# Six slices of w_in shared by three groups, and PSUM as two rings of two, in a retention and SiLU kernel

## The chip, the cores and the metric

The kernel runs on one core of one Trainium2 chip. The time is the device time of the core in microseconds, and lower is better. Three runs of the kernel before gave 663.20, 664.37 and 661.12 us, so its median is 663.2 us.

## The reference

The first part is a recurrent retention over 4 batches, 8 heads, 768 positions and a head dimension of 64. The second part is a dense block with a SiLU between two products, over 3072 tokens of width 512, with an inner width of 2048.

```python
gamma = 1.0 - 2.0 ** (-5.0 - np.arange(H))
for t in range(S):
    state = gamma * state + einsum('bhd,bhe->bhde', k[:, :, t], v[:, :, t])
    y[:, :, t] = scale * einsum('bhd,bhde->bhe', q[:, :, t], state)
x = y.transpose(0, 2, 1, 3).reshape(B * S, H * D)
h = x @ w_in
g = h * (1.0 / (1.0 + np.exp(-h)))
out = g @ w_out
```

## The kernel before

**Retention in chunks.** The 768 positions are cut into 6 chunks of 128. One chunk of one batch is a unit, so there are 24 units, taken in the order of chunks. A unit passes through three steps on TensorE, at three successive visits. `stage_t` transposes k and q into PSUM, and ACT copies them out as `kt` and `qt`. `stage_a` forms the scores `sc` from them, and VectorE multiplies these by the decay into `am`. `stage_y` forms the unit's output y from v and `am` and from q and the running state, and adds k times v to the state. So visit m does the transpositions of unit m, y of unit m - 2 and the scores of unit m - 1, in that order. `finish_y` and `split_x` then turn y into x of the dense block. All the x of one chunk, for its four batches, is a group of 512 tokens.

**Three-term products.** The dense products run in the fp32r format. Each operand is held as three parts: a high part, a low part, and a mix of both. In the code these are indices 0, 1 and 2. A product of x and a slice of w_in is 12 matmuls: for each of the four parts of the inner dimension, high by high and low by low go to the accumulator `ha`, and mix by mix goes to `hb`. At the end ACT takes `ha` into a tile of the pool `hpool`, VectorE subtracts `hb`, ACT applies the SiLU, and the tile g is stored to DRAM.

**The slices of w_in.** There are 16 slices of 128 columns (index f). The weights come as 64-bit words. `take_w` takes the next slice: it asks for a load two slices ahead, converts the words to 32 bits on VectorE and ACT (`convert_w`), and splits the result in three (`split_w`). After the 16 slices of w_in it goes on with the 16 slices of w_out, which are only converted and stored to DRAM. The output stage needs them later.

**The order of the work.** Six visits come first, with four slices. Then a list of phases says which groups use which slices. Groups 0 and 1 use slices 0 to 7 in turn, then group 0 and group 1 use slices 8 to 15. Between the products the list places the takes of slices and the visits. Groups 2 to 5 then go over all 16 slices each, with visits and w_out conversions in between. The output stage reads g back from DRAM, splits it in three (`split`), and multiplies it by w_out with eight accumulators, two for each batch.

**Group 2's x.** The pool `xpool` has two places. Group 2's x (`LATE`) is made while groups 0 and 1 hold both. So `finish_y` copies y of this chunk to an SBUF tile `ys` and stores it to DRAM, and `late_x` loads it back (`yr`) and splits it. The four calls of `late_x` stand after products (1, 9), (1, 10), (1, 11) and (1, 12). The tiles `ys`, `yr` and g share the three buffers of `hpool`, tag `hs`.

**PSUM.** The eight banks are cut up by name. The pool `ps_u` has one buffer each for `s` (two banks, for the transposed k and for the scores), `q` (one bank, for the transposed q) and `y` (two banks). The pool `ps_h` has three banks that `ha` and `hb` take in turn.

**What sets the order.** TensorE does its instructions in the order in which the program is written. For the other engines a scheduler places the instructions, and each engine then does its own in that order, one after another. Loads and stores are issued by SyncE, also in order. Each waits at the head of its queue until its buffer is free and its data is ready. The helper `issue_after` keeps a slice's first ACT step behind a named earlier ACT instruction.

The code around the change follows, with the line numbers that the profile uses.

Of the kernel before, what the change touches and what calls it, by code (L numbers as in the profile page):

```python
# [31 lines left out]
def kernel(  # L32
# [53 lines left out]
    hpool = pool("hpool", 3)  # L86
    stage = pool("stage", 2)
    conv = pool("conv", 1)
    ps_u = pool("ps_u", 1, space=PS)
    ps_h = pool("ps_h", 3, space=PS)  # L90

    g_dram = {(c, f): dram.tile([128, NT], FP32, tag=f"g{c}_{f}", name=f"gd_{c}_{f}")
              for c in range(NC) for f in range(NF)}
# [3 lines left out]
    def bits(x):  # L97
        return float(np.array(x, np.uint32).view(np.float32))

    def split_w(f, w32, name, factor):  # L100

        w = wpool.tile([128, 3, 512], FP32R, tag=f"w{f}", name=f"{name}{f}")
        lo = conv.tile([128, 512], FP32, tag="wl", name=f"{name}l_{f}")
        with tc.issue_after(evac[0]):
            nc.scalar.activation(out=w[:, 0, :], in_=w32, func=AF.Copy, scale=HALF * factor)
        high = w[:, 0, :].bitcast(FP32)
        nc.vector.scalar_tensor_tensor(out=lo, in0=w32, scalar=factor, in1=high,
                                       op0=ALU.mult, op1=ALU.subtract)
        nc.scalar.activation(out=w[:, 1, :], in_=lo, func=AF.Copy, scale=1.0 / EPS)
        nc.vector.scalar_tensor_tensor(out=w[:, 2, :], in0=high, scalar=EPS, in1=lo,  # L110
                                       op0=ALU.mult, op1=ALU.subtract)
        return w
# [73 lines left out]
        nc.vector.tensor_tensor(out=w, in0=s.bitcast(FP32), in1=p.bitcast(FP32), op=ALU.add)  # L186
        return w

    evac, w_sb = [], {}
    taken = [0]  # L190

    def take_w(between=lambda: None):
# [69 lines left out]

    xt, kt, qt, am, live = {}, {}, {}, {}, {}

    def banks(tag, name, n=2):
        return ps_u.tile([128, n, 512], FP32, tag=tag, name=name)

    def turn(name):  # L270
        return ps_h.tile([128, 512], FP32, tag="h", name=name)

    def scale_k(n):
        if 0 <= n < len(units) and units[n][0] < NC - 1:
# [9 lines left out]

    def stage_t(n):

        kp = turn(f"kp_{n}") if n < B + 2 else banks("s", f"kp_{n}")[:, 0]
        qp = banks("q", f"qp_{n}", 1)[:, 0]
        for (name, to, bufs), src, tp in ((("kt", kt, 2), kqv["k"][n], kp),
                                          (("qt", qt, 3), kqv["q"].pop(n), qp)):  # L290
            tp = tp.rearrange("p (a t) -> p a t", a=HP)
            for a in range(HP):
                nc.tensor.transpose(tp[:, a, :], src[:, 2 * a : 2 * a + 2, :], ident)  # L293
            to[n] = one.tile([128, HP, C], FP32, tag=name, name=f"{name}_{n}", bufs=bufs)
            evac[:] = [nc.scalar.copy(out=to[n], in_=tp).ins]

    def stage_y(n):

        c, b = units[n]
        kf, vs = kqv["k"].pop(n), kqv["v"].pop(n)  # L300
        qtn, amn = qt[n], am.pop(n)
        u = banks("y", f"y_{n}")

        yp = u[:, :, : 2 * C].rearrange("p o (i t) -> p i o t", i=2)
        sp = u[:, 1, 2 * C :].rearrange("p (a e) -> p a e", a=HP)

        started = set()

        def product(j, bank, **kw):
            nc.tensor.matmul(start=(j, bank) not in started, skip_group_check=True, **kw)  # L310
# [13 lines left out]
        if c > 0:  # L324
            for i in range(0, HP, 2):
                for a in (i, i + 1):
                    for j in range(2):
                        o = j ^ (a % 2)
                        product(o, a % 2, out=yp[ts(o, D), a // 2, a % 2, :],
                                lhsT=state[b][ts(j, D), a, :], rhs=qtn[ts(j, D), a, :],  # L330
                                stop=True)
        live[n] = sp, yp

    def stage_a(n):

        u = banks("s", f"sc_{n}").rearrange("p j (a t) -> p j a t", a=HP)
        ktn = kt.pop(n)
        for a in range(HP):
            for j in range(2):
                for half in range(2):  # L340
                    nc.tensor.matmul(u[ts(half, D), j, a, :], lhsT=ktn[ts(j, D), a, ts(half, D)],  # L341
                                     rhs=qt[n][ts(j, D), a, :], start=True, stop=True,
                                     skip_group_check=True)
        am[n] = one.tile([128, 2, HP, C], FP32, tag="am", name=f"am_{n}")
        nc.vector.tensor_tensor(out=am[n], in0=u, in1=decay, op=ALU.mult)

    def finish_y(n):
        c, b = units[n]
        sp, yp = live.pop(n)
        qt.pop(n)  # L350
        if b == 0 and c != LATE:
            xt[c] = xpool.tile([128, 3, KIN, NT], FP32R, tag="xt", name=f"xt_{c}")
        if c == LATE:
            y = hpool.tile([128, KIN, C], FP32, tag="hs", name=f"ys_{b}")
            nc.scalar.copy(out=y.rearrange("p (i o) t -> p i o t", o=2), in_=yp)
            nc.sync.dma_start(out=y_dram[b], in_=y)
            rest = None
        else:
            rest = split_x(c, b, yp)
        if c == 0:  # L360
            nc.scalar.copy(out=state[b], in_=sp)
        elif c < NC - 1:
            nc.vector.tensor_tensor(out=state[b], in0=state[b], in1=sp, op=ALU.add)
        return rest

    def split_x(c, b, y):
        xh, xl, xm = (xt[c][:, i, :, ts(b, C)].rearrange("p (i o) t -> p i o t", o=2)
                      for i in range(3))
        nc.scalar.activation(out=xh, in_=y, func=AF.Copy, scale=HALF)
        nc.vector.tensor_tensor(out=xl, in0=y, in1=xh.bitcast(FP32), op=ALU.subtract)  # L370
        return lambda: nc.vector.scalar_tensor_tensor(
            out=xm, in0=xl.bitcast(FP32), scalar=-1.0 / EPS, in1=xh.bitcast(FP32),
            op0=ALU.mult, op1=ALU.add)


    LATE = 2
# [32 lines left out]
    pending = []  # L409

    def product_in(c, f):
        ha, hb = turn(f"ha_{c}_{f}"), turn(f"hb_{c}_{f}")
        for i in range(3):
            for kk in range(KIN):
                nc.tensor.matmul(hb if i == 2 else ha, lhsT=w_sb[f][:, i, ts(kk, 128)],  # L415
                                 rhs=xt[c][:, i, kk, :], start=kk == 0 and i != 1,
                                 stop=kk == KIN - 1 and i != 0)
        hs = hpool.tile([128, NT], FP32, tag="hs", name=f"g_{c}_{f}")
        nc.scalar.activation(out=hs, in_=ha, func=AF.Copy, scale=ONE_E)  # L419
        nc.vector.tensor_tensor(out=hs, in0=hs, in1=hb, op=ALU.subtract)  # L420
# [54 lines left out]
    for m in range(1, B + 2):  # L475
# [2 lines left out]
            take_w()  # L478
        if m == 2:
            first_chunk()  # L480
    half = NF // 2
    phases = ((0, 0, (0, 1, 2, 3, 5), (0, 1, 2, 3, 4, 5, 6)),
              (1, 0, (1, 3, 5), (0, 1, 2, 3, 5)),
              (0, half, (), (2, 6)),
              (1, half, (), (7,)))
    for c, f0, at, takes in phases:
        for i in range(half):
            product_in(c, f0 + i)
            if i in takes:
                take_w()  # L490
            put_g(1)
            if i in at:
                visit()
            if (c, f0) == (1, half) and 1 <= i <= B:
                late_x(i - 1)
    for c in range(2, NC):
        for f in range(NF):
            product_in(c, f)
            if c < NC - 1 and f % 3 == 0:
                take_w()  # L500
            put_g(1)
            if f % 4 == 1:
                visit()
            if c == NC - 1:
                if f == 0:
                    get_w(0)
                    get_w(1)
                wo[f] = split_w(f, w_got.pop(f), "wo", 1.0)
                get_w(f + 2)
                if f >= NF - 6:  # L510
                    if f == NF - 6:
                        for n in range(G_AHEAD):
                            get(n)
                    if f >= NF - S_AHEAD:
                        split(f - NF + S_AHEAD)
    put_g(0)

    for c in range(NC):
        acc = []
        for b in range(B):  # L520
            if b < 2:
                u = banks("sy"[b], f"o{b}_{c}")
                acc.append([u[:, i] for i in range(2)])
            else:
                acc.append([turn(f"oa{b}_{c}"), turn(f"ob{b}_{c}") if b == 2 else
                            banks("q", f"ob{b}_{c}", 1)[:, 0]])
        for f in range(NF):
            n = c * NF + f
            split(n + S_AHEAD)
# [45 lines left out]
```

## Time and profile before

| what | value |
|---|---|
| median of three runs | 663.2 us |
| the profiled execution, its time | 663.2 us |
| the profiled execution, its span | 661.1 us |
| TensorE matmul (PE) busy | 630.0 us, 95% |
| TensorE weight load (PEld) busy | 517.8 us, 78% |
| VectorE (DVE) busy | 422.4 us, 64% |
| ScalarE (ACT) busy | 283.1 us, 43% |
| granted TensorE clock, mean | 0.99 |
| DMA, mean | 157 GB/s |

The span is the stretch from the first to the last instruction of the profiled execution. Busy times of engines overlap, so they do not add up. In the lists of waits a line names the waiting instruction, the instruction or transfer that released it, the total in microseconds, how often it was seen, and the longest. In a timeline a line has the start, the time taken, the engine, the line of the code and the operation, and in square brackets the idle time before it and what ended it. Matmuls are pipelined, so that the time from the start of one to the start of the next is shorter than what is given as the duration of one.

### The profile page before, as it was taken

What the parts mean: (1) busy time and instruction counts of PE and PEld (TensorE: products, weight loads), DVE (VectorE), ACT (ScalarE), POOL (GpSimd) and SP (SyncE); (2) the same over time, 40 slices, a digit from 0 to 9 for tenths busy, and PEclk for the clock granted to TensorE, in tenths of its full rate; (3) what the DMA queues carried; (4) which work ended last, traced back from release to release, by engine and by line L of the source; (5) the groups of instructions that cost most, each with busy time, mean ns of one, the idle gap of its engine ahead of it and who ended that gap; (6) DMA issues with size and microseconds to landing.
All of it is one profiled execution on the core that took longest, in us unless ns stands there. A gap on an engine that the chain in (4) does not pass through costs nothing.

```text
span 661.1 us, 11067 instructions
## 1 busy us (share of the span) xinstructions
PE 630.0 (95%) x4288; PEld 517.8 (78%) x4288; DVE 422.4 (64%) x696; ACT 283.1 (43%) x510; POOL 12.6 (2%) x44
## 2 busy tenths in 40 slices
PE   3878979899999999999999999999999999999996
PEld 2667758688888888888888888888888888888885
DVE  4999998995568787864348775454464545554631
ACT  5465546564554444444438881222131412222311
POOL 3000100100000000000000000000000000000000
PEclk9989989999999999999999999999999999999999
DMA  8957866867457775864326654252343443423401
GB/s 192 226 129 200 205 199 194 222 223 223 144 168 218 197 216 160 243 205 160 128 81 191 195 181 134 77 179 81 110 146 110 130 126 95 160 95 96 153 7 63
DMA packets 123060, 103.48 MB, mean 157 GB/s; under 512 B 80000, under 2 KB 88192, under 8 KB 123008
## 3 DMA queue, kind: packets, MB, share of 16 engines
q1 hardware_dynamic: 119552, 96.49, 49.9%
q10 hardware_dynamic: 3456, 6.29, 2.6%
q8 instruction: 33, 0.54, 0.3%
q14 instruction: 19, 0.16, 0.1%
HBM read 66.06 MB, written 36.70 MB: 155 GB/s over the span
## 4 chain that ended last, share of the span: by engine, by line
PE 73%; DVE 0%; ACT 0%; issue 0%; ACTq 0%
PE ha L415 18%; PE hb L415 9%; PE ob L537 7%; PE o L536 7%; PE o L537 7%; PE o L535 7%; PE oa L536 7%; PE oa L535 7%; PE y L310 4%; PE sc L341 1%; PE kp L293 1%; PE qp L293 1%; DVE o L543 0%; ACT o L542 0%; ACT g L419 0%
## 5 line engine op out<-in xcount | busy, mean ns | idle before, releaser
L415 PE MATMUL ha<-xt,wi 128*128 128x512 f32 x768 | 192.9, 393 | 2.9 <-DVE g L420 2.9
L415 PEld LDWEIGHTS ha<-xt,wi 128*128 128x128 f32 x768 | 142.4, 188 | 36.3 <-DVE g L420 3.7
L462 DVE TENSOR_TENSOR gs<-gr,gs 128x512 fp32r<-128x512 f32 x96 | 62.1, 686 | 93.8 <-ACT gs L460 93.8
L460 ACT ACTIVATE gs<-gr 128x512 fp32r<-128x512 f32 x96 | 53.5, 620 | 139.7 <-issue 131.8
L415 PE MATMUL hb<-xt,wi 128*128 128x512 f32 x384 | 104.0, 393 | 3.1 <-ACT g L419 3.0
L420 DVE TENSOR_TENSOR g<-g,hb 128x512 f32<-128x512 f32 x96 | 65.7, 684 | 60.8 <-PE hb L415 43.5
L421 ACT ACTIVATE g<-g 128x512 f32<-128x512 f32 x96 | 60.5, 632 | 70.9 <-DVE g L420 69.2
L415 PEld LDWEIGHTS hb<-xt,wi 128*128 128x128 f32 x384 | 72.3, 189 | 19.3 <-ACT g L419 4.4
L537 PE MATMUL ob<-wo,gs 128*128 128x512 f32 x192 | 75.2, 392 | 0.0
L536 PE MATMUL o<-wo,gs 128*128 128x512 f32 x192 | 74.7, 389 | 0.0
L537 PE MATMUL o<-wo,gs 128*128 128x512 f32 x192 | 74.7, 389 | 0.0
L535 PE MATMUL o<-wo,gs 128*128 128x512 f32 x192 | 74.7, 389 | 0.0
L535 PE MATMUL oa<-wo,gs 128*128 128x512 f32 x192 | 74.7, 389 | 0.0
L536 PE MATMUL oa<-wo,gs 128*128 128x512 f32 x192 | 74.7, 389 | 0.0
L419 ACT ACTIVATE g<-ha 128x512 f32<-128x512 f32 x96 | 56.6, 589 | 40.1 <-PE ha L415 33.3
L463 DVE SCALAR_TENSOR_TENSOR gs<-gs 128x512 fp32r<-128x512 f32 x96 | 61.9, 684 | 0.0
L537 PEld LDWEIGHTS ob<-wo,gs 128*128 128x128 f32 x192 | 36.0, 188 | 9.0 <-DVE o L543 1.7
L535 PEld LDWEIGHTS oa<-wo,gs 128*128 128x128 f32 x192 | 36.0, 188 | 7.7 <-ACT o L542 0.2
L537 PEld LDWEIGHTS o<-wo,gs 128*128 128x128 f32 x192 | 36.0, 188 | 7.5
L536 PEld LDWEIGHTS o<-wo,gs 128*128 128x128 f32 x192 | 36.0, 188 | 7.5
L536 PEld LDWEIGHTS oa<-wo,gs 128*128 128x128 f32 x192 | 36.0, 188 | 7.4
L535 PEld LDWEIGHTS o<-wo,gs 128*128 128x128 f32 x192 | 36.0, 188 | 7.3
(65 smaller groups left out, 612.8 us busy)
## 6 DMA issues: line engine op xcount, KB each, us to landing
gd<-g SPq DMA_DIRECT2D x96, 256.0 KB, 3.1
gr<-gd SPq DMA_DIRECT2D x96, 256.0 KB, 2.7
wf<-in_moe_w_out_dram SPq DMA_DIRECT2D x16, 512.0 KB, 3.9
kf<-in_k_dram SPq DMA_DIRECT2D x24, 256.0 KB, 4.5
qf<-in_q_dram SPq DMA_DIRECT2D x24, 256.0 KB, 4.5
vf<-in_v_dram SPq DMA_DIRECT2D x24, 256.0 KB, 4.5
out_dram<-o ACTq DMA_DIRECT2D x24, 256.0 KB, 2.1
wf<-in_moe_w_in_dram SPq DMA_DIRECT2D x16, 256.0 KB, 3.2
```

The costliest lines, as they stand in the source:

```text
L293: nc.tensor.transpose(tp[:, a, :], src[:, 2 * a : 2 * a + 2, :], ident)
L310: nc.tensor.matmul(start=(j, bank) not in started, skip_group_check=True, **kw)
L415: nc.tensor.matmul(hb if i == 2 else ha, lhsT=w_sb[f][:, i, ts(kk, 128)], rhs=xt[c][:, i, kk, :], start=kk == 0 and i != 1, stop=kk == KIN ...
L419: nc.scalar.activation(out=hs, in_=ha, func=AF.Copy, scale=ONE_E)
L420: nc.vector.tensor_tensor(out=hs, in0=hs, in1=hb, op=ALU.subtract)
L421: nc.scalar.activation(out=hs, in_=hs, func=AF.Silu)
L460: nc.scalar.activation(out=t[:, 0, :], in_=g, func=AF.Copy, scale=HALF)
L462: nc.vector.tensor_tensor(out=t[:, 1, :], in0=g, in1=high, op=ALU.subtract)
L463: nc.vector.scalar_tensor_tensor(out=t[:, 2, :], in0=t[:, 1, :].bitcast(FP32), scalar=-1.0 / EPS, in1=high, op0=ALU.mult, op1=ALU.add)
L535: nc.tensor.matmul(oa, lhsT=gh, rhs=wo[f][:, 0, :], start=first_, stop=False)
L536: nc.tensor.matmul(oa, lhsT=glo, rhs=wo[f][:, 1, :], start=False, stop=last)
L537: nc.tensor.matmul(ob, lhsT=gm, rhs=wo[f][:, 2, :], start=first_, stop=last)
```

## The change

**PSUM.** `ps_u` becomes one tag `u` of two banks with two buffers, which the transpositions of k and q together, the scores and y take in turn. `ps_h` gets the tags `ha` and `hb`, with two buffers each. The output stage takes its accumulators from these.

**Products.** The 12 matmuls are issued with the part of the inner dimension outermost: two on `ha`, one on `hb`, and so on.

**Slices.** The last four slices share one tile, `wq`, of four places. Group 2's x stands in this tile first: `finish_y` still copies y to `ys` and stores it to DRAM, and it now also splits it into the tile. The slices that come into the tile follow the products that read x from it.

**Order.** A dictionary `steps` gives for each product whether a slice is taken and whether a visit follows. Groups 0, 1 and 2 use slices 0 to 5, groups 0 and 1 slices 6 to 10, groups 0 and 1 slices 11 to 15, and group 2 slices 6 to 15. The four calls of `late_x` stand after products (1, 12) to (1, 15).

```diff
-    ps_u = pool("ps_u", 1, space=PS)
-    ps_h = pool("ps_h", 3, space=PS)
+    ps_u = pool("ps_u", 2, space=PS)
+    ps_h = pool("ps_h", 2, space=PS)
...
+    def w_slot(f, name):
+        if f < NF - 4:
+            return wpool.tile([128, 3, 512], FP32R, tag=f"w{f}", name=f"{name}{f}")
+        if f == NF - 4:
+            quads[name] = wpool.tile([128, 4, 3, 512], FP32R, tag="wq", name=f"{name}4")
+        return quads[name][:, f - NF + 4]
...
-        w = wpool.tile([128, 3, 512], FP32R, tag=f"w{f}", name=f"{name}{f}")
+        w = w_slot(f, name)
...
-        with tc.issue_after(evac[0]):
+        with tc.issue_after(held[0] if f >= NF - 4 else evac[0]):
...
-    def banks(tag, name, n=2):
-        return ps_u.tile([128, n, 512], FP32, tag=tag, name=name)
-
-    def turn(name):
-        return ps_h.tile([128, 512], FP32, tag="h", name=name)
+    def banks(name):
+        return ps_u.tile([128, 2, 512], FP32, tag="u", name=name)
...
-        kp = turn(f"kp_{n}") if n < B + 2 else banks("s", f"kp_{n}")[:, 0]
-        qp = banks("q", f"qp_{n}", 1)[:, 0]
-        for (name, to, bufs), src, tp in ((("kt", kt, 2), kqv["k"][n], kp),
-                                          (("qt", qt, 3), kqv["q"].pop(n), qp)):
-            tp = tp.rearrange("p (a t) -> p a t", a=HP)
+        tp = banks(f"tp_{n}").rearrange("p o (a t) -> p o a t", a=HP)
+        for i, src in enumerate((kqv["k"][n], kqv["q"].pop(n))):
             for a in range(HP):
-                nc.tensor.transpose(tp[:, a, :], src[:, 2 * a : 2 * a + 2, :], ident)
+                nc.tensor.transpose(tp[:, i, a, :], src[:, 2 * a : 2 * a + 2, :], ident)
+        for i, (name, to, bufs) in enumerate((("kt", kt, 2), ("qt", qt, 3))):
             to[n] = one.tile([128, HP, C], FP32, tag=name, name=f"{name}_{n}", bufs=bufs)
-            evac[:] = [nc.scalar.copy(out=to[n], in_=tp).ins]
+            evac[:] = [nc.scalar.copy(out=to[n], in_=tp[:, i]).ins]
...
-        if b == 0 and c != LATE:
-            xt[c] = xpool.tile([128, 3, KIN, NT], FP32R, tag="xt", name=f"xt_{c}")
+        if b == 0:
+            p, tag = (wpool, "wq") if c == LATE else (xpool, "xt")
+            xt[c] = p.tile([128, 3, KIN, NT], FP32R, tag=tag, name=f"xt_{c}")
         if c == LATE:
             y = hpool.tile([128, KIN, C], FP32, tag="hs", name=f"ys_{b}")
-            nc.scalar.copy(out=y.rearrange("p (i o) t -> p i o t", o=2), in_=yp)
+            y4 = y.rearrange("p (i o) t -> p i o t", o=2)
+            nc.scalar.copy(out=y4, in_=yp)
             nc.sync.dma_start(out=y_dram[b], in_=y)
-            rest = None
-        else:
-            rest = split_x(c, b, yp)
+            yp = y4
+        rest = split_x(c, b, yp)
...
-        ha, hb = turn(f"ha_{c}_{f}"), turn(f"hb_{c}_{f}")
-        for i in range(3):
-            for kk in range(KIN):
-                nc.tensor.matmul(hb if i == 2 else ha, lhsT=w_sb[f][:, i, ts(kk, 128)],
-                                 rhs=xt[c][:, i, kk, :], start=kk == 0 and i != 1,
-                                 stop=kk == KIN - 1 and i != 0)
+        ha = ps_h.tile([128, 512], FP32, tag="ha", name=f"ha_{c}_{f}")
+        hb = ps_h.tile([128, 512], FP32, tag="hb", name=f"hb_{c}_{f}")
+        for kk in range(KIN):
+            w = [w_sb[f][:, i, ts(kk, 128)] for i in range(3)]
+            x = [xt[c][:, i, kk, :] for i in range(3)]
+            first_, last = kk == 0, kk == KIN - 1
+            nc.tensor.matmul(ha, lhsT=w[0], rhs=x[0], start=first_, stop=False)
+            nc.tensor.matmul(ha, lhsT=w[1], rhs=x[1], start=False, stop=last)
+            nc.tensor.matmul(hb, lhsT=w[2], rhs=x[2], start=first_, stop=last)
...
-    phases = ((0, 0, (0, 1, 2, 3, 5), (0, 1, 2, 3, 4, 5, 6)),
-              (1, 0, (1, 3, 5), (0, 1, 2, 3, 5)),
-              (0, half, (), (2, 6)),
-              (1, half, (), (7,)))
...
-            if (c, f0) == (1, half) and 1 <= i <= B:
-                late_x(i - 1)
...
+    for c, f, takes, at in ((0, range(6), (0, 2, 5), (0, 1, 3, 4)),
+                            (1, range(6), (2, 5), (0, 1, 3, 4)),
+                            (2, range(6), (1, 4), ()),
+                            (0, range(6, 11), (7, 9), ()),
+                            (1, range(6, 11), (7, 9), ()),
+                            (0, range(11, NF), (11, 13), ()),
+                            (1, range(11, NF), (), ()),
+                            (2, range(6, NF), (6, 9, 12, 15), (6, 8, 11, 13))):
+        for i in f:
+            steps[c, i] = i in takes, i in at
+    for c in range(3, NC):
+        for f in range(NF):
+            steps[c, f] = c < NC - 1 and f % 3 == 0, f % 4 == 1
+    for (c, f), (takes, at) in steps.items():
+        product_in(c, f)
+        if takes:
+            take_w()
+        put_g(1)
+        if at:
+            visit()
+        if c == 1 and NF - B <= f:
+            late_x(f - NF + B)
...
-                u = banks("sy"[b], f"o{b}_{c}")
+                u = banks(f"o{b}_{c}")
                 acc.append([u[:, i] for i in range(2)])
             else:
-                acc.append([turn(f"oa{b}_{c}"), turn(f"ob{b}_{c}") if b == 2 else
-                            banks("q", f"ob{b}_{c}", 1)[:, 0]])
+                acc.append([ps_h.tile([128, DM], FP32, tag=f"h{i}", name=f"o{i}{b}_{c}")
+                            for i in "ab"])
```

More of the change, by code (lines that the diff above doesn't have):

```diff
@@ L98, in bits @@
         return float(np.array(x, np.uint32).view(np.float32))
+    quads = {}
+    def w_slot(f, name):
[4 more added lines that the diff above has]
+        return quads[name][:, f - NF + 4]
     def split_w(f, w32, name, factor):
-        w = wpool.tile([128, 3, 512], FP32R, tag=f"w{f}", name=f"{name}{f}")
+        w = w_slot(f, name)
         lo = conv.tile([128, 512], FP32, tag="wl", name=f"{name}l_{f}")
-        with tc.issue_after(evac[0]):
+        with tc.issue_after(held[0] if f >= NF - 4 else evac[0]):
             nc.scalar.activation(out=w[:, 0, :], in_=w32, func=AF.Copy, scale=HALF * factor)
@@ L187, in convert_w @@
         return w
-    evac, w_sb = [], {}
+    evac, held, w_sb = [], [], {}
     taken = [0]
@@ L301, in stage_y @@
         qtn, amn = qt[n], am.pop(n)
-        u = banks("y", f"y_{n}")
+        u = banks(f"y_{n}")
         yp = u[:, :, : 2 * C].rearrange("p o (i t) -> p i o t", i=2)
@@ L334, in stage_a @@
     def stage_a(n):
-        u = banks("s", f"sc_{n}").rearrange("p j (a t) -> p j a t", a=HP)
+        u = banks(f"sc_{n}").rearrange("p j (a t) -> p j a t", a=HP)
         ktn = kt.pop(n)
@@ L368, in split_x @@
                       for i in range(3))
-        nc.scalar.activation(out=xh, in_=y, func=AF.Copy, scale=HALF)
+        held[:] = [nc.scalar.activation(out=xh, in_=y, func=AF.Copy, scale=HALF).ins]
         nc.vector.tensor_tensor(out=xl, in0=y, in1=xh.bitcast(FP32), op=ALU.subtract)
@@ L480 @@
             first_chunk()
-    half = NF // 2
-    phases = ((0, 0, (0, 1, 2, 3, 5), (0, 1, 2, 3, 4, 5, 6)),
-              (1, 0, (1, 3, 5), (0, 1, 2, 3, 5)),
-              (0, half, (), (2, 6)),
-              (1, half, (), (7,)))
[L486 to L493, printed above, removed]
-            if (c, f0) == (1, half) and 1 <= i <= B:
-                late_x(i - 1)
@@ L496 @@
-    for c in range(2, NC):
-        for f in range(NF):
[L498 to L515, printed above, removed]
+    steps = {}
@@ new lines @@
+    for c in range(3, NC):
+        for f in range(NF):
+            steps[c, f] = c < NC - 1 and f % 3 == 0, f % 4 == 1
[8 more added lines that the diff above has]
+            late_x(f - NF + B)
+        if c == NC - 1:
+            if f == 0:
+                get_w(0)
+                get_w(1)
+            wo[f] = split_w(f, w_got.pop(f), "wo", 1.0)
+            get_w(f + 2)
+            if f >= NF - 6:
+                if f == NF - 6:
+                    for n in range(G_AHEAD):
+                        get(n)
+                if f >= NF - S_AHEAD:
+                    split(f - NF + S_AHEAD)
```

## The prediction

> **What bounds the kernel now.** I read the page's slices first, then TensorE's waits by stretch, then the timelines where they fall.
>
> ```profile
> PE   3878979899999999999999999999999999999996
> DVE  4999998995568787864348775454464545554631
> PEclk9989989999999999999999999999999999999999
> ```
>
> Each digit is 16.5 us. TensorE is full from about 130 us on; its holes lie in the first eight slices, where VectorE stands at 9. From 175 us to the end no matmul is listed as waiting. So only what happens before about 130 us can be gained, and whatever stalls TensorE later is lost whole. The waits of TensorE between 33 and 131 us:
>
> ```profile
> PE ha L415 <- DVE g L420: 2.9, 2, 1.5
> PE hb L415 <- ACT g L419: 2.9, 1, 2.9
> PE kp L293 <- DVE am L345: 2.7, 3, 1.1
> PE y L310 <- ACT state L361: 2.6, 1, 2.6
> PE y L310 <- DVE am L345: 1.0, 1, 1.0
> PE sc L341 <- ACT kt L295: 0.3, 2, 0.2
> ```
>
> They all end on ACT or VectorE emptying a bank. What one wait costs shows in TensorE's timeline:
>
> ```profile
> 91.28 1.97 PE L415 MATMUL ha<-xt,wi 128*128 128x512 f32 x8
> 96.13 2.08 PE L415 MATMUL hb<-xt,wi 128*128 128x512 f32 x4 [2.88 <-ACT g L419]
> 98.00 1.06 PE L293 MATMUL kp<-ident,kf 128*128 128x128 f32 x4
> ...
> 113.33 2.11 PE L415 MATMUL ha<-xt,wi 128*128 128x512 f32 x8
> 115.28 1.07 PE L415 MATMUL hb<-xt,wi 128*128 128x512 f32 x4
> ```
>
> After the 2.88 us hole four matmuls take 2.08 us in place of 1.07, and the small ones are slow until about 102.3: some 6.2 us at half rate, about 3.1 us lost on top of the hole. After the hole at 33 to 37 us it is 3.5 us at half rate.
>
> Units of account. In the full stretch a product (12 matmuls) starts every 2.72 us (147.32, 150.04, 152.76). An attention visit adds 4.10 us: hb ends at 180.43 and the product after next starts at 187.25, 6.82 less 2.72. Before, products run from 40.94, and at 130.86 there are 16 products and 8 visits done: 16 x 2.72 + 8 x 4.10 = 76.3 us of work in 89.9. **13.6 us is lost there, and that is all that the front can give.** VectorE explains it: 8 slices of w_in are made ready for the first 8 products. By the pitch of the timeline (0.60 us for a 128x512 of two operands, 0.34 for one, 1.13 for am, 0.33 for state) a slice costs it 4.0 us, a visit 3.9, a product 0.6: 8.5 us for one of each, against 6.8 on TensorE.
>
> Last, the reload of group 2's x, which now has cover:
>
> ```profile
> 163.04 0.69 DVE L370 TENSOR_TENSOR xt<-yr,xt 128x512 fp32r<-128x512 f32 x1 [0.73 <-ACT xt L369]
> ...
> 172.53 0.69 DVE L371 SCALAR_TENSOR_TENSOR xt<-xt 128x512 fp32r<-128x512 f32 x1
> ```
>
> Its fourth part is asked for after product (1,12), which ends at 166.4, and is ready at 173.2: 6.8 us later. Group 2 starts at 174.99, because three products stand in between.
>
> **What the Trainium skill says.** "TensorE: Matmul & The Clock Gate", Part 1, gives half rate after an idle window of about 3.4 us and full rate after a busy one, with a free-running window; the 3.5 and 6.2 us above agree, and say that the cost can be one or two windows. "ScalarE: Activation LUTs", What ACT_TABLE_LOAD costs, gives 1283 ns and a drain of 1380; the trace shows 1.28 us at 45.10 and the next activation at 46.39, so no drain is counted. "DMA: Bandwidth & Descriptors", Anatomy of one DMA, gives about 2 us fixed, so a store followed by a load cannot be short; the trace has 2.7 us median for yr and 3.1 for gd.
>
> **The change, part by part.**
>
> *Order of products: six slices shared by groups 0, 1, 2.* Slices needed early fall from 8 in 16 products to 6 in 18; takes are spread at about one per 2 to 3 products. VectorE per visit and product without a slice is 4.5 us against 6.8. So the standing shortage goes. The same 18 products and 8 visits ended before at 130.86 + 2 x 2.72 = 136.3; without stalls they need 81.8 from 40.94, which is 122.7. New stalls in this stretch:
>
> S1. In the changed program VectorE does am of unit 4 (1.13), a step of slice 3 (0.6) and scale_q (0.6) ahead of the last xm of group 0; before, xm was done at 41.94, ahead of am at 42.46. And the product now takes kk outermost, so its third matmul wants xm, not its ninth. Tp, sc and y share two buffers, so a transposition waits for the state copy of the y two visits back, with no product between in the prologue. Walking the prologue with the durations above: state copies let the transposition of visit 5 go at about 35.7 (before 32.1), y of unit 3 ends at 39.7, am at 42.9, xm at 45.0. The third matmul wanted 41.4: **3.6 us**.
>
> S2. sc of the first visit in group 0 needs qt's copy too (same buffer), which ACT does behind the table load (1.28) and the silu (0.63), and this waits for the subtraction, queued on VectorE behind all of slice 4 (5.1 us chained). sc then starts at about 53.4 where 50.2 is wanted: **3.2 us**, with the half rate after S1 inside it. Later visits: product end E, ha copy to E+0.5, subtraction to E+1.3, silu to E+1.95, qt to E+2.5, sc wanted at E+2.94: covered by y's own 2.1 us, by 0.4. Where a slice step stands in front (visits 8 and 10) I count 0.7 + 1.0 = **1.7 us**.
>
> S3. x of group 2 is now also split at once, from ys; xm stands behind am and scale_q, with one product of cover (2.72): ready about 5.1 after y, wanted at 4.2: **1.0 us**.
>
> Sum 9.5: the 18 products end at 132.2, a **gain of 4.1 us** (13.6 at most).
>
> *Double ha, hb in place of three in turn; banks alternating.* This removes the four waits of hb/ha on g (5.8 us, part of the 13.6). The output stage already alternates banks and runs 12 matmuls per 2.72 us: nothing for the alternation.
>
> *x of group 2 in place of the last four slices.* The spill to DRAM and the reload stay: 4 stores, 4 loads, none saved. ACT and VectorE gain 4 splits (0.63 + 0.69 + 0.69 each, 8.0 us in all), in the stretch just counted. The four slices wait for (2,5); they are wanted from (0,12), over seven products later: covered. The four last wo slices wait likewise for (5,15), and are wanted 12 output steps later, 32 us: covered.
>
> *Reload at f = 12 to 15.* The SyncE order is the same as before, shifted by three products: gd 11, yr, gd 12, yr, gd 13, gd 14, yr, yr. But product (2,6) follows (1,15) at once, where three products (8.2 us) stood. The last yr needs the slot of g(1,14), hence its store landed. Taking the measured chain over: xm ready 6.8 us after (1,15), wanted 0.45 after: **6.4 us**. Bounds: 5.5 if stores land in 2.0; 9 if each takes 3.1, since ACT now places the second yr's xh ahead of silu 14. A hole of 6 us puts the clock at half: 3.5 to 6.2 us of it, 1.7 to 3.1 lost, I take **2.4**. Together **8.8 us**; TensorE has nothing else to do there, its order is written by hand. Behind it q, k, v of later visits wait too, but they have three visits of lead.
>
> *The 12 later visits* with sc behind qt: cover 0.4 us each; bounds 0 and 8, I take **0.5**.
>
> Net: -4.1 + 8.8 + 0.5 = **+5.2 us**: span 666.3. The profiled execution took 663.2 with a span of 661.1, and the median is 663.2 too, so the time is 668.4, in round numbers 668; a slowdown of 0.8%. 0.5%, 3.3 us, is about what can be told from no change.
>
> **Rivals.** *Faster:* the front loses only S1 (3.6): it gains 13.6 - 3.6 = 10.0; the reload costs its lower bound of 5.5 and 0.5 of clock, 6.0: 663.2 - 10.0 + 6.0 = 659.2. For it: all prices of S2 hang on queue order, and half rate may fall inside work that waits anyway. Against: the reload chain is measured. It decides once the front's gain exceeds the reload by 3.3. *A wash:* front gain 7, reload 8: 664. *The ring becomes the bound:* sc waits for qt in most visits, 0.6 us in 16 more of the 24: 668.4 + 9.6 = 678. For it: the cover is 0.4 us and ACT is in order. Against: in the full stretch before, qt's copy ends at 182.66 and sc starts at 183.37.
> *No effect of the sharing:* if the k, q, v transfers set the pace (196 GB/s in 41 to 131 us, 226 at most), the front gains nothing and the time is 672; no such wait is listed after 20 us.
>
> **How the numbers follow.** Forecast case (664.5 to 672.5) 0.54; wash 0.18; faster 0.15; ring or transfers 0.13. The range takes in half of the fast case and of the slow one: 660 to 675. Faster by over 0.5%: 0.14; within: 0.25; slower: 0.61, from forecast and ring, less the forecast's edge below 666.5.
>
> **What would show it.** Product (2,6) starts, and its third matmul waits 5 to 9 us for xm of the last yr, with a slow clock after; the first product waits some 3 us for xm; waits of kp on am vanish; sc on ACT's qt appears. (2,5) ends at about 132. Wrong if (2,6) waits under 3 us, or if (2,5) ends before 127 or after 137.

## The result and the profile after

The changed kernel takes **671.9 us** (671.19 to 673.08), against 663.79 us (661.12 to 664.95) for the kernel before on the same chip: a ratio of **1.013** (95% interval 1.0094 to 1.0166), 8.1 us slower. The forecast was 668.0, with 660 to 675 as its range. The profiled execution took 671.3 us with a span of 669.4, so the span grew by 8.3 us where the working had +5.2.

The slices of the span, as on the page before (one digit is now 16.7 us):

```profile
PE   3769999999979999999999999999999999999996
DVE  4897888999546776868667759363545454544631
PEclk9879999999979999999999999999999999999999
```

VectorE reads 7, 8, 8 in the fourth to the sixth slice, where it stood at 9, and TensorE reaches 9 in the fourth slice and stays there up to the twelfth, where before it fell back to 7 or 8 as late as the eighth. That is the front's gain. The third slice got worse: 6 for 7, with 7 for 8 in the granted clock. In the twelfth slice, where before both read 9, there is a 7, with a 7 below it for the granted clock: a new hole with a slow stretch. The list of TensorE's waits over the whole span (total us, times, longest), without those for the loads of k, q and v (11.9 us, before 10.8, all in the first 33 us):

```profile
PE hb L425 <- DVE xt L375: 5.0, 2, 3.5
PE ha L423 <- ACT xt L373: 4.9, 1, 4.9
PE tp L295 <- ACT state L365: 4.0, 3, 2.3
PE sc L344 <- ACT qt L298: 3.9, 6, 1.1
PE y L313 <- DVE am L348: 0.9, 2, 0.6
```

All waits of products for g are gone but one of 0.2 us, and so are those of transpositions for am. In their place stand the products' waits for x, and sc's wait for the copy of qt. The state copy, for which y waited 3.7 us before, is now waited for by the transpositions. TensorE's timeline where these fall (start, us, instruction, idle time before it and what ended it):

```profile
45.23 0.51 PE L425 MATMUL hb<-xt,wi 128*128 128x512 f32 x1 [3.53 <-DVE xt L375]
...
53.42 1.10 PE L344 MATMUL sc<-qt,kt 64*64 64x128 f32 x32 [1.06 <-ACT qt L298]
70.93 1.10 PE L344 MATMUL sc<-qt,kt 64*64 64x128 f32 x32 [0.97 <-ACT qt L298]
88.36 1.10 PE L344 MATMUL sc<-qt,kt 64*64 64x128 f32 x32 [0.87 <-ACT qt L298]
...
117.92 0.50 PE L425 MATMUL hb<-xt,wi 128*128 128x512 f32 x1 [1.47 <-DVE xt L375]
...
188.09 0.39 PE L425 MATMUL hb<-xt,wi 128*128 128x512 f32 x1
193.37 0.79 PE L423 MATMUL ha<-xt,wi 128*128 128x512 f32 x1 [4.89 <-ACT xt L373]
194.10 0.79 PE L424 MATMUL ha<-xt,wi 128*128 128x512 f32 x1
194.82 0.80 PE L425 MATMUL hb<-xt,wi 128*128 128x512 f32 x1
195.42 0.63 PE L423 MATMUL ha<-xt,wi 128*128 128x512 f32 x1
```

The first product of the kernel waits at its third matmul (45.23), the first product of group 2 does so at 117.92, and (2,6) follows (1,15) after a hole of 4.89 us. Its first three matmuls come one by one, 0.73 us apart, as xh, xl and xm are made; the rest run with 0.63 us each where 0.39 is the rule.

The time can be laid out from a few marks in the two timelines. The first 18 products and 8 visits end at 133.9 (before at 136.3, as the prediction worked it out; the timeline has 136.4): 2.4 us gained. The third matmul of (2,6) starts at 194.82 in place of 188.77, 6.05 us late; the ten matmuls from it take 4.44 us in place of 2.27, and the transposition behind them is 0.27 us longer: 2.4 us of slow clock. The output stage starts at 401.9 (before 393.5) and lasts 267.5 us (before 267.6), so nothing happens there. That leaves 8.3 + 2.4 - 6.05 - 2.4 = 2.3 us for the 12 visits that follow (2,6).

### The profile page after: what moved, and what is told of

Read it like the earlier page. It is cut to its first block, busy times and chain, and to the rows that moved or that the text cites. A ratio compares the mean times of both kernels' runs of the same rounds, so it can differ in the third digit from the quotient of the medians.

```text
span 669.4 us, 11108 instructions
## 1 busy us (share of the span) xinstructions
PE 633.0 (95%) x4288; PEld 518.9 (78%) x4288; DVE 430.4 (64%) x704; ACT 284.1 (42%) x514; POOL 10.1 (2%) x44
## 4 chain that ended last, share of the span: by engine, by line
PE 80%; DVE 3%; ACT 3%; DMA 2%; issue 1%; ACTq 0%; SPq 0%; DVEq 0%
PE ha L423 12%; PE hb L425 11%; PE ha L424 11%; PE ob L547 7%; PE o L545 6%; PE o L546 6%; PE o L547 6%; PE oa L545 6%; PE oa L546 6%; PE y L313 3%; PE sc L344 2%; PE tp L295 1%; DMA yr<-yd 1%; DVE g L428 1%; ACT g L429 1%
## 5 line engine op out<-in xcount | busy, mean ns | idle before, releaser
L423 PE MATMUL ha<-xt,wi 128*128 128x512 f32 x384 | 153.5, 400 | 4.9 <-ACT xt L373 4.9
L425 PE MATMUL hb<-xt,wi 128*128 128x512 f32 x384 | 151.7, 395 | 5.2 <-DVE xt L375 5.0
L424 PE MATMUL ha<-xt,wi 128*128 128x512 f32 x384 | 151.4, 394 | 0.0
L423 PEld LDWEIGHTS ha<-xt,wi 128*128 128x128 f32 x384 | 72.7, 189 | 23.2 <-ACT xt L373 5.3
L424 PEld LDWEIGHTS ha<-xt,wi 128*128 128x128 f32 x384 | 72.9, 190 | 15.4 <-DVE xt L374 0.7
L547 PEld LDWEIGHTS o<-wo,gs 128*128 128x128 f32 x192 | 36.0, 188 | 7.5
L545 PEld LDWEIGHTS oa<-wo,gs 128*128 128x128 f32 x192 | 36.0, 188 | 7.5
L546 PEld LDWEIGHTS o<-wo,gs 128*128 128x128 f32 x192 | 36.0, 188 | 7.5
```

The costliest lines, as they stand in the source:

```text
L423: nc.tensor.matmul(ha, lhsT=w[0], rhs=x[0], start=first_, stop=False)
L424: nc.tensor.matmul(ha, lhsT=w[1], rhs=x[1], start=False, stop=last)
L425: nc.tensor.matmul(hb, lhsT=w[2], rhs=x[2], start=first_, stop=last)
L545: nc.tensor.matmul(oa, lhsT=gh, rhs=wo[f][:, 0, :], start=first_, stop=False)
L546: nc.tensor.matmul(oa, lhsT=glo, rhs=wo[f][:, 1, :], start=False, stop=last)
L547: nc.tensor.matmul(ob, lhsT=gm, rhs=wo[f][:, 2, :], start=first_, stop=last)
```

## Experiments

"Changed" below is the changed kernel, 671.9 us and span 669.4. Ratios are to the kernel before on the same chip. Its median there lay between 663.44 and 663.79 us, so times of different chips are set against each other as they are.

### Where the loss sits: one cause taken away at a time

**The reload left out.** Group 2 reads group 1's x from slice 6 on, so that part of its product is left out of the computation and another, of the same size, put in.

```
-            x = [xt[c][:, i, kk, :] for i in range(3)]
+            x = [xt[1 if c == 2 and f >= 6 else c][:, i, kk, :] for i in range(3)]
...
-        if c == 1 and NF - B <= f:
-            late_x(f - NF + B)
```

> The changed kernel without the reload of group 2's x: late_x is left out and group 2's products from slice 6 on read group 1's x, which is still in place, so the matmuls are as many and the four loads and four splits are gone. If the reload is what TensorE stands for at (2,6) (6.05 us of waiting and 2.4 us at half rate, as the trace after shows), the time falls by 8.4 us, to 663.5. If something else is late at that place too (the slices, the banks, the stores of g), the hole stays in part and the time stays above 667.

Measured: 663.95 us, ratio 1.000 (0.9986 to 1.0015), span 662.1. The hole and its slow clock are worth 8.0 us by the medians, 7.3 by the spans. (By the spans it is a little less than the 8.45 of the timeline: the later visits lose 1.0 us more in this run.) So the reload costs about as much as the whole distance to the kernel before, 8.1 us, and the 2.4 us that the front gains are eaten by the later visits.

**Part outermost again in the product**, with the two rings kept:

```
-        for kk in range(KIN):
...
-            nc.tensor.matmul(hb, lhsT=w[2], rhs=x[2], start=first_, stop=last)
+        for i in range(3):
+            for kk in range(KIN):
+                nc.tensor.matmul(hb if i == 2 else ha, lhsT=w_sb[f][:, i, ts(kk, 128)],
...
```

> The changed kernel with the 12 matmuls of a product in the old order (the part outermost, hb last), the rings of banks kept. If xm is what the third matmul waits for at (0,0), (2,0) and (2,6), hb now wants it 1.4 us later in each: 2.1, 0.1 and about 5 us remain of 3.5, 1.5 and 6.05, the ha of a product is free 0.9 us earlier so that qt's copy comes earlier and the waits of sc fall from 6 us in all to under 3; together 4 to 6 us, to 667. If the order of the matmuls has nothing to do with it, or alternating banks gained something in every product, the time is 672 or more.

Measured: 666.07 us, ratio 1.004 (1.0028 to 1.0052), span 664.1: 5.8 us less than the changed kernel. The xm of group 0 is waited for by the ninth matmul now:

```profile
44.38 2.05 PE L421 MATMUL hb<-xt,wi 128*128 128x512 f32 x4 [2.67 <-DVE xt L375]
```

The wait of 1.47 us at (2,0) is not listed any more; the reload's hole is (4.1 us, for xh). Up to the transpositions behind (2,6) the reload now costs 6.85 us in place of 8.45. The order of the twelve matmuls, which changes no work at all, thus sets whether a late third part of x is seen. The other half of what was expected did not come: the waits of sc did not fall, 5.1 us are listed where the changed kernel has 3.9.

**xm ahead of am on VectorE** (the other cause of the same waits):

```
-            rest = finish_y(m - 2)
+            finish_y(m - 2)()
...
-        if rest is not None:
-            rest()
```

> The changed kernel with xm ahead of am in the program, so that VectorE does xm before am and scale_q. If the queue on VectorE is what made the first product and (2,0) wait, the waits of 3.5 and 1.5 us for xm fall to about 1.5 and 0 (am 1.13, scale_q 0.6 and a slice step gone from in front), with less at half rate: 668. The hole at (2,6) stays at 6 us. If the prologue's waits on the state copies set it, the 3.5 us stays.

Measured: 666.57 us, ratio 1.005 (1.0028 to 1.0072), span 664.4: 5.3 us less. More than was expected: with the wait goes the slow clock behind it.

```profile
42.39 0.50 PE L422 MATMUL hb<-xt,wi 128*128 128x512 f32 x1 [0.90 <-DVE xt L375]
```

The 3.53 us are down to 0.90, and the wait at (2,0) is gone.

**silu placed behind the copies of kt and qt** where a visit follows:

```
-        nc.scalar.activation(out=hs, in_=hs, func=AF.Silu)
+        later.append(hs)
...  (silu() does this activation behind stage_t of the visit, or at once where none follows)
```

> The changed kernel with one order changed on ACT: where a visit follows a product, the silu of that product stands behind the copies of kt and qt, not between them. If sc waits because qt's copy stands behind a silu that waits for VectorE's subtraction, the waits of sc on qt (3.9 us listed, and some 0.3 us more at each of six later visits) vanish with what half rate they leave: 671.9 falls by 4 to 6, to 667. If sc waits because the copies come late anyway (ACT full), the time is within 1 us of 671.9.

Measured: 666.14 us, ratio 1.0034 (1.0019 to 1.0049), span 664.2: 5.7 us less. From the start of a visit's transpositions to its sc, the rule is 2.94 us (2.48 in the last chunk). Summed over the 18 visits between 40 and 340 us that show it all, the changed kernel loses 4.1 us on that in the front and 2.4 behind (2,6), 6.5 in all; this run loses 1.55, all in the front, and nothing behind. The waits of sc that remain:

```profile
PE sc L344 <- ACT qt L298: 1.0, 3, 0.4
```

Why the copy of qt came late shows in ACT's timeline of the changed kernel, at the first visit of group 0:

```profile
50.37 0.58 ACT L298 COPY kt<-tp 128x512 f32<-128x512 f32 x1 [0.16 <-PE tp L295]
50.97 1.28 ACT L429 ACT_TABLE_LOAD   x1
52.27 0.63 ACT L429 ACTIVATE g<-g 128x512 f32<-128x512 f32 x1
52.80 0.57 ACT L298 COPY qt<-tp 128x512 f32<-128x512 f32 x1
```

Between the two copies stand the table load and the silu. The subtraction that this silu reads (VectorE, 50.19, 0.68 us) was done before the copy of kt was, so ACT does not stand still here: the copy of qt is late by the 1.83 us of work in front of it. The Trainium skill, "Perfetto Trace Analysis", Tensor Engine Instruction, says that ACT and VectorE take their instructions strictly in order; this trace agrees: by the timeline the transposed q was there at 50.28, and its copy came behind the load and the silu, at 52.80. At a visit behind (2,6), where sc waits 0.51 us, ACT does stand still for VectorE:

```profile
231.37 0.63 ACT L429 ACTIVATE g<-g 128x512 f32<-128x512 f32 x1 [2.71 <-DVE g L428]
231.91 0.58 ACT L427 ACTIVATE g<-ha 128x512 f32<-128x512 f32 x1
232.39 0.58 ACT L298 COPY kt<-tp 128x512 f32<-128x512 f32 x1
233.25 0.63 ACT L429 ACTIVATE g<-g 128x512 f32<-128x512 f32 x1 [0.28 <-DVE g L428]
233.78 0.57 ACT L298 COPY qt<-tp 128x512 f32<-128x512 f32 x1
```

The silu between the copies waits 0.28 us for its subtraction. The silu of the product before waited 2.71 us and so made everything behind it late, the copy of kt too. It does so at the visits of 66.84 and 84.37 as well (2.09 and 1.94 us), where two steps of a slice stand ahead of the copies too. There the run with the silu moved takes only one silu out of the way, and 0.45 and 0.40 us of the waits of sc stay. In the kernel before, sc used another buffer than qp and did not ask for that copy.

### The two halves of the change

**The new order alone**, with PSUM and the products as before:

```
-    ps_u = pool("ps_u", 2, space=PS)
-    ps_h = pool("ps_h", 2, space=PS)
+    ps_u = pool("ps_u", 1, space=PS)
+    ps_h = pool("ps_h", 3, space=PS)
...  (banks, turn, stage_t, product_in and the output's accumulators as before)
```

> Only the order of groups and slices, the shared tile and the place of the reload; PSUM and the products as before. If the gain of sharing six slices is real and the two rings ate it, (0,0) goes at about 41 as before, the front gains 8 to 10 us by (2,5), and the reload takes back about 7.5: 662. If the front's gain was small because VectorE or the transfers set the pace whatever the banks, (2,5) ends at 133 and the time is about 669.

Measured: 662.72 us, ratio 0.9984 (0.9972 to 0.9997), span 661.3. There is no wait of sc, and (2,5) ends at 126.2 (the last visit's sc starts at 105.70, the first of the seven products behind it at 106.68, the eighth at 126.22): the front gains 10.1 us with this order. The reload takes more than half of it back:

```profile
180.90 1.07 PE L425 MATMUL hb<-xt,wi 128*128 128x512 f32 x4
186.11 3.68 PE L425 MATMUL ha<-xt,wi 128*128 128x512 f32 x8 [4.14 <-ACT xt L378]
189.63 1.09 PE L425 MATMUL hb<-xt,wi 128*128 128x512 f32 x4
```

4.14 us of hole, and 3.68 us for eight matmuls that take 1.98 elsewhere: 5.8 us, or 6.0 from the start of one matmul to the start of the next. Up to the output stage another 2.4 us go in small waits; it starts at 391.8, 1.7 us earlier than before. The output stage itself is 1.9 us longer than before, with 1.3 us of waits for ACT to empty the accumulators that the kernel before does not show; why it waits there was not looked into. In the changed kernel the place of the reload costs 8.45, 2.45 more: x comes 0.75 us later, the first three matmuls wait for xh, xl and xm one by one (1.0), where here only the ninth needs xm, and the slow clock takes 0.7 more.

**The rings and the new products alone**, on the order, slices and reload of before:

```
-    ps_u = pool("ps_u", 1, space=PS)
-    ps_h = pool("ps_h", 3, space=PS)
+    ps_u = pool("ps_u", 2, space=PS)
+    ps_h = pool("ps_h", 2, space=PS)
...  (banks, stage_t, product_in and the output's accumulators as in the change; phases as before)
```

> Only the two rings of PSUM and the products by parts of the inner dimension; order of groups, slices and reload as before. If the rings cost what the prediction gave them, (0,0) ends 3 to 5 us later, the waits of ha and hb on g (5.8 us, and 3.1 at half rate) are gone, sc waits some 2 us in the visits before 130 us and 2 after: 665, about 1 to 3 us slower than before. If the rings are free, 655, and if they are the whole loss, 672.

Measured: 669.94 us, ratio 1.0092 (1.0063 to 1.012), span 667.8. This was a miss: some 5 us more than expected.

```profile
PE sc L336 <- ACT qt L290: 8.0, 6, 2.3
PE tp L287 <- ACT state L356: 3.9, 3, 2.3
PE hb L415 <- DVE xt L366: 3.5, 1, 3.5
```

Where slices of w_in are still made ready close together, the wait of sc is larger (8.0 us against 3.9), as the subtraction that silu waits for is queued behind them: ahead of the longest wait of sc, 2.26 us, ACT stands still for it for 2.42 us. So the rings with the new products, not the order of the groups, are what costs: +6.5 us on the old order, and on the new one 671.9 - 662.7 = 9.2. The 2.7 us between these is about the 2.45 by which the reload's hole is dearer with them; on the old order the reload has cover and no such hole.

On the new order the two can be told apart, for the run with the part outermost differs from the order alone by the rings only. The rings cost 666.1 - 662.7 = 3.4 us there, and the order of the twelve matmuls on top of them 671.9 - 666.1 = 5.8, the larger share. For the old order no run parts them.

**The rings with silu behind the copies**, on the order of before (the move of the silu from above, made in the kernel with the rings and the new products alone):

> The same order on ACT in the kernel with the two rings alone (order of groups as before), where sc waits 8.0 us on qt. The same reason gives 669.9 less 8 to 10: 661, a little faster than before, since the waits of ha and hb on g are gone. If instead the rings cost by the first product and by the tie of transpositions to the state copies, it stays at 667 or more.

Measured: 666.94 us (665.03 to 669.5), ratio 1.0054 (1.0037 to 1.0071), span 663.4: 3.0 us less than the rings alone, but 6 above what was expected. sc still waits 4.1 us, in three visits. ACT's timeline ahead of the longest of them (sc starts at 86.03, after 2.00 us):

```profile
83.34 0.63 ACT L412 ACTIVATE g<-g 128x512 f32<-128x512 f32 x1 [1.77 <-DVE g L426]
83.88 0.58 ACT L425 ACTIVATE g<-ha 128x512 f32<-128x512 f32 x1
84.36 0.58 ACT L290 COPY kt<-tp 128x512 f32<-128x512 f32 x1
84.82 0.68 ACT L172 ACTIVATE ca<-wf 128x512 f32<-128x512 f32 x1
85.39 0.59 ACT L290 COPY qt<-tp 128x512 f32<-128x512 f32 x1
```

The silu that holds ACT here belongs to the product before the visit's own, and a step of a slice stands between the copies. With VectorE more than a product late, moving one silu is not enough. That is read from the trace, not tried.

### Cover for the reload

**Groups 0 and 1 whole, the reload early** (on the order alone): group 0 on slices 6 to 15, then group 1, with the reload asked for at (1,6) to (1,9), six products ahead of (2,6). Slices 11 to 15 have to be ready earlier for it.

```
-                            (2, range(6), (1, 4), ()),
-                            (0, range(6, 11), (7, 9), ()),
-                            (1, range(6, 11), (7, 9), ()),
-                            (0, range(11, NF), (11, 13), ()),
-                            (1, range(11, NF), (), ()),
+                            (2, range(6), (1, 3, 5), ()),
+                            (0, range(6, NF), (6, 8, 9, 11), ()),
+                            (1, range(6, NF), (), ()),
...
-        if c == 1 and NF - B <= f:
-            late_x(f - NF + B)
+        if c == 1 and 6 <= f < 6 + B:
+            late_x(f - 6)
```

> PSUM and products as before, the new order of groups, but group 0 goes through slices 6 to 15 and then group 1 through 6 to 15, with the reload after (1,6) to (1,9), six products ahead of (2,6); slices 11 to 15 are taken earlier for it. If the hole at (2,6) is the missing cover, it is gone (4.1 us of waiting and about 3 at half rate or for xl): 662.7 less 7, 656. If the earlier slices cost VectorE as much as the cover gives, some 3 us come back as waits of group 0 on slices 13 to 15: 659. If the reload is slow whatever its place, 662.

Measured: 663.01 us, ratio 0.9987 (0.9973 to 1.0002), span 661.2. A miss, though the hole at (2,6) is gone:

```profile
156.29 1.21 PE L425 MATMUL ha<-xt,wi 128*128 128x512 f32 x4 [3.04 <-ACT wi L115]
157.69 1.64 PE L425 MATMUL ha<-xt,wi 128*128 128x512 f32 x4 [0.18 <-ACT wi L119]
```

A slice is late instead, 3.04 us, and a slow clock comes with it. The wait moved.

**The tail split in another place** (on the order alone), so that the slices are needed as late as before the experiment and three products stand between the last part of the reload and (2,6):

```
-                            (1, range(6, 11), (7, 9), ()),
+                            (1, range(6, 9), (7, 8), ()),
                             (0, range(11, NF), (11, 13), ()),
-                            (1, range(11, NF), (), ()),
+                            (1, range(9, NF), (), ()),
...
-        if c == 1 and NF - B <= f:
-            late_x(f - NF + B)
+        if c == 1 and 9 <= f < 9 + B:
+            late_x(f - 9)
```

> The order alone (the run e3: 662.7 us, span 661.3) with only the tail of groups 0 and 1 arranged again: group 0 on slices 6 to 10, group 1 on 6 to 8, group 0 on 11 to 15, group 1 on 9 to 15, and late_x after the products (1,9) to (1,12), so that three products (13 to 15, some 11 us) stand between the last read of the second buffer's batch and (2,6), as before. Theory (the reload's place at the very end of group 1 is what loses the gain of the front): the 4.1 us wait of the first product of (2,6) and the half rate behind it go, 655 to 658 us. Rival (as in the run e6, the cover is eaten by slices that come late to the products ahead): a wait on slices 14 or 15 takes its place, 661 to 664 us.

Measured: 659.32 us (657.12 to 660.38), ratio **0.9917** (0.9884 to 0.995), span 655.0. The hole is gone, and of TensorE's waits between 150 and 215 us two are left, on the copy of ha:

```profile
169.67 1.19 PE L425 MATMUL hb<-xt,wi 128*128 128x512 f32 x4 [0.71 <-ACT g L429]
176.19 1.20 PE L425 MATMUL hb<-xt,wi 128*128 128x512 f32 x4 [0.79 <-ACT g L429]
```

The median gained 3.4 us on the order alone, the profiled span 6.3; the range of 3.3 us over four runs leaves the size uncertain between these, the sign not.

**The same tail in the changed kernel**, with its rings (the same edit as above):

> The changed kernel (671.9 us) with only the same tail (group 0 on 6 to 10, group 1 on 6 to 8, group 0 on 11 to 15, group 1 on 9 to 15, late_x after (1,9) to (1,12)). Leaving the reload out gave 8.0 us; with three products of cover the same 8 should come with the reload in place: 663 to 666 us. Rival (the slices or the stores come late under this order): 668 to 671 us.

Measured: 664.04 us, ratio 1.0004 (0.9988 to 1.002), span 661.8: 7.9 us less than the changed kernel, as much as leaving the reload out. No wait of TensorE is listed between 150 and 215 us. So the cost of the reload was its place in the order, not its work.

**All three mends**: that tail, silu behind the copies, xm ahead of am, on the changed kernel with its rings and its products.

> The changed kernel with its two rings kept and three mends at once: that tail, silu placed behind the copies of kt and qt where a visit follows, and xm computed right behind the subtraction of xl. Alone they gave 8.0 (the reload left out), 5.7 and 5.3 us. If they add up: 653 us. Some of each was the half rate after a stall and the wait of xm that the second mend made longer, so the likelier is 655 to 659 us, below both kernels. Rival (the mends compete for the same order on VectorE and ScalarE, each wait taking the place of another): 661 to 665 us.

Measured: **656.02 us** (655.52 to 656.08), ratio **0.987** (0.9844 to 0.9896), span 654.1. It beats both kernels: 7.5 us below the one before and 15.9 below the changed one. The three gains apart are 7.9, 5.7 and 5.3, in sum 18.9, of which 15.9 came. TensorE's waits between 33 and 131 us:

```profile
PE tp L295 <- ACT state L365: 2.3, 1, 2.3
PE y L313 <- DVE am L348: 1.4, 2, 0.9
PE hb L430 <- DVE xt L375: 1.2, 1, 1.2
PE sc L344 <- ACT qt L298: 1.0, 3, 0.5
```

5.9 us, where the kernel before lists 12.4 in that stretch; between 140 and 190 us 0.3 is listed, and from there to the output stage nothing. The output stage starts at 386.6 (before 393.5, changed 401.9). The longest wait left is the transposition's for the state copy two visits back, 2.3 us; before, it was y that waited for that copy, 2.6 us.

## Why the prediction was right, and where it was off

Point by point, by its own steps:

- **The slowdown, its sign and its main cause: right.** The reload at (2,6) was put at 6.4 us of wait and 2.4 of slow clock; the timeline shows 6.05 and 2.4. Leaving it out gave 8.0 us, and covering it 7.9. The other signs that were named came too: no wait of transpositions for am, sc behind qt, and (2,5) at 133.9 where about 132 was said.
- **S1, the first product's wait for xm: right.** Third matmul forecast at 45.0, found at 45.23; wait 3.6, found 3.53. The cause is shown: xm ahead of am on VectorE leaves 0.90, and the products with the part outermost see 2.67.
- **S2, sc behind the copy of qt at the first visit: right,** at 53.4 and found at 53.42, by the queue on ACT that was named. One link of it was not seen: the subtraction ended at 50.87, in time, so the table load and the silu alone made the copy late. For the next visits with a slice step in front I had 1.7 us; the stretches from transposition to sc show 1.15, 1.05 and 0.35, in sum 2.55.
- **S3, xm at (2,0):** 1.0 forecast, 1.47 found.
- **The front's gain: 4.1 forecast, 2.4 found.** The slice-step term of S2 was too small by 0.85 and S3 by 0.47: 1.3 of the 1.7 us. (The 0.2 us by which S1 came later is made up by the first sc, at 53.42.) The other 0.4 is not assigned. That more was to be had is shown by the order alone, with 10.1 of the 13.6 us.
- **"The 12 later visits: cover 0.4 us each, I take 0.5": the other term that was mis-sized, by 1.6 us.** The stretch from transposition to sc is longer than before by 0.69, 0.29, 0.08, 0.30, 0.49 and 0.24 us in six of the twelve, in sum 2.1 (and 0.27 in the first, from the slow clock). The cover of 0.4 us was worked out for a VectorE that does the subtraction at once; at the visit of 230.77 it had a step of w_out in hand for 1.41 us, and the silu of the product before waited 2.71. This is a part of the rival "the ring becomes the bound", which had the right mechanism and put it at 9.6 us; with silu behind the copies all of the 2.1 is gone.
- **Rings at nothing, or a gain of the four waits on g: wrong as a sum.** The waits on g did go (5.8 us in the kernel before). But the same edit brought S1, S2 and the waits of the later visits, so that alone it costs 6.5 us. The prediction set S1 and S2 against the gain of the order; the runs show that they belong to the rings and the new products, for they come with the old order too (xm 3.5 us, the first sc 1.06) and are not there with the order alone.
- **The rival "a wash"** missed by the front: it wanted a gain of 7 there. **The rival "faster"** asked for a front that loses only S1 and a reload at its lower bound, 10.0 and 6.0 us; the order alone has 10.1 and 5.8, and still comes to 662.7 by its small waits and a longer output stage. With cover for the reload it is the version at 0.9917. **"No effect of the sharing"** gave 672, near the measured time, but not for its reason: waits for k, q and v stand in the first 33 us alone, and the front did gain.

Net, in the prediction's terms: -2.4 + 8.45 + 2.1 = +8.15, of 8.3 found. The forecast of +5.2 was short by 1.7 in the front and 1.6 in the later visits, and 0.35 too high at the reload. So it is not right by errors that cancel.

## What to carry to other kernels

When buffers are merged into one ring, ask of every user of the ring whose copy it now waits for, and what stands ahead of that copy on its in-order engine: here a table load, and silus that themselves wait for VectorE. When a loop's order is changed, ask which operand it now wants first: the third part of x, made last and wanted by the third matmul in place of the ninth, was worth 5.8 us. When work is taken out of an order, look at what it was covering: the three products between the reload and its reader were worth 8 us. Three small changes of order, with no work removed, turned 1.3% slower into 1.3% faster.

## What had not been expected of the hardware

How long the clock stays at half after a hole does not go by the hole's length. 4.14 us of hole were followed by about 3.6 us at half rate (the order alone), 4.89 us by about 6.5 (changed), and in the kernel before 2.88 us by 6.2. In the rings alone a hole of 2.26 us was followed by 3.4 us at half rate: the sc behind it took 1.98 us in place of 1.05. Nor does the same hole cost the same: behind the transposition's wait of 2.33 us at 35.54 the changed kernel has some 3.3 us at half rate (y takes 1.66 us), and with the part outermost the same wait at 35.25 has none (y takes 1.04). The Trainium skill, "TensorE: Matmul & The Clock Gate", Part 1, speaks of a free-running window of about 3.4 us; one or two such windows at half rate come near these lengths, as the prediction said of its 3.5 and 6.2 us. But holes of 2.26 and 2.88 us are shorter than a whole idle window, and the measurement decides: such holes can cost clock too.
